# Attention scores without a wide reciprocal, a first chunk that starts its MLP alone, and weights fetched from the beginning

## The chip, the cores and the metric

The kernel runs on one core of one Trainium2 chip. The metric is device time in microseconds (us) of one execution; lower is better. All times are medians of runs in the fast state on the chip (an execution over 1.5% above the fastest of its kernel would be left out), each with runs of the kernel before beside it.

## The reference

An attention layer with a decaying state (RWKV-6) for 4 sequences, 8 heads, 768 steps, head size 48, and after it an MLP with a hard-swish gate:

```python
for t in range(S):                       # per batch and head
    cur = outer(u * k_t, v_t)
    y_t = r_t @ (state + cur)
    state = w_t[:, None] * state + outer(k_t, v_t)
x = y, heads side by side                # (3072, 384)
h = x @ w_in                             # (384, 2048)
g = h * clip(h + 3, 0, 6) / 6
out = g @ w_out                          # (2048, 384)
```

## The kernel before

The steps are cut into 24 chunks of 128 (6 to a sequence). Within a chunk the products of decays turn the recurrence into matrix products: R = r times the decay up to the step, K = k divided by the decay up to and with the step, and the scores are K against R. Three chunks make a block of 384 columns (the tile xT) for the MLP, with 16 up projections ("ups", three matmuls of 384 columns each, then a gate on ScalarE and VectorE) and 12 quarters of a down projection. The weights arrive as 64-bit words and are converted on ScalarE and VectorE, in pairs of 128-column slices: 16 conversions. PSUM is the memory that the matmuls write their results to. All this is interleaved; in each built program every engine has its own fixed list of instructions.

```python
def weights(which, f):                         # fetch a pair and convert it
    ...
    bits = io.tile([128, n], I64, name="bits", bufs=3)
    ...                                        # two DMAs on SyncE's queue
    nc.scalar.activation(out=more, in_=lo, ...)          # 2 on ScalarE
    nc.scalar.activation(out=more.bitcast(I32), in_=more, ...)
    nc.vector.tensor_scalar(out=top, in0=hi, ...)        # 3 on VectorE
    nc.vector.scalar_tensor_tensor(out=top, in0=hi, ...)
    nc.vector.tensor_tensor(out=dst, in0=top, in1=more.bitcast(I32), op=ALU.add)

def prep(i):
    d = st[i]
    W_ = wk.tile([PR, P * (L + 1)], F32, name="W")
    nc.vector.tensor_tensor_scan(out=W_, data0=d["w"], data1=restart..., op0=ALU.mult, op1=ALU.add)
    ...
    nc.vector.reciprocal(out=inv, in_=W[:, :, 1:])       # 112 x 512
    ...
    nc.gpsimd.tensor_mul(R, d["r"], W[:, :, :L])
    nc.gpsimd.tensor_mul(K, d["k"], inv)
    ...                                        # rk on GpSimd, dg on VectorE, A on ScalarE

def up(bk, f):
    h_ps = pp.tile([128, MB], F32, name="mm", bufs=4)    # one of four PSUM buffers
    for j in range(NCC):
        nc.tensor.matmul(h_ps, lhsT=w_in[:, f, j, :], rhs=b["xT"][:, j, :], ...)
    r6 = wk.tile([128, MB], F32, name="r6", bufs=3)
    nc.scalar.activation(out=r6, in_=h_ps, func=ACT.Relu, bias=half, scale=1.0 / 6.0)
    nc.vector.scalar_tensor_tensor(out=g, in0=r6, scalar=1.0, in1=h_ps, op0=ALU.min, op1=ALU.mult)

def attend(i, some=lambda n: None):            # score: K against R, then the mask on VectorE
    score(i); turn_k(i); some(3); write(i); some(1); read(i)   # some(n): n pieces of the MLP

prep(0); prep(1); attend(0); prep(2); attend(1); attend(2)
first = pieces_of(0)                           # 16 ups, 12 quarters of a down
...                                            # 3 conversions ahead of the first up, the rest spread over the ups
todo.extend(first)
load(3); prep(3)
...
for i in range(BC, NT):
    left = max(0, (i - BC + 1) * per_block // BC - lag - done)   # lag = 5
    ...
    load(i + 1); attend(i, some); prep(i + 1); some(left)
```

## Time and profile before

| | before |
|---|---|
| median of 3 runs | 647.87 us (647.71 to 648.11) |
| span of the profiled run | 647.6 us (a run of 649.35 us), mean granted clock 0.982 |
| TensorE busy | 609.8 us (94%) |
| VectorE busy | 318.8 us (49%) |
| GpSimd busy | 135.7 us (21%) |

The prediction below shows the slices, the timeline and the stretches. Two more views are needed later. First the groups of instructions of the page: line, engine, operation, tiles written and read, count, then busy time and mean ns of one, then idle time of the engine before them and what ended it.

```profile
L211 DVE RECIPROCAL inv<-W 112x512 f32<-112x512 f32 x24 | 80.4, 3349 | 0.6
...
L215 POOL TENSOR_TENSOR K<-feat_in,inv 112x512 f32<-112x512 f32 x24 | 31.1, 1296 | 57.9 <-DVE inv L211 36.1
```

The wide reciprocal costs 3.35 us a chunk, a quarter of VectorE's busy time, and GpSimd's K waits for it. The second view is what TensorE waited for in the first 125 us (us in total, times, longest).

```profile
PE a_ps L234 <- POOL K L215: 17.8, 3, 15.5
```

Of 17.8 us for K, 15.5 are the start of the program.

### The profile page before, as it was taken

How to read it: one execution, taken by the hardware profiler on the slowest of the kernel's cores; microseconds unless marked ns; L12 is line 12 of the kernel's file. 1: busy time of each engine (PE TensorE's matmuls, PEld its weight loads, DVE VectorE, ACT ScalarE, POOL GpSimd, SP SyncE). 2: the span in 40 equal slices, each digit the busy share in tenths (PEclk: the TensorE clock that was granted, in tenths of full speed). 3: DMA queues.
4: the chain of work that ended last, by engine and by line, in shares of the span. 5: the costliest groups of instructions: out<-in, count | busy, mean ns of one | idle time of the engine just before them, and what ended most of it. 6: DMA issues, size and time to landing. Idle time of an engine off the chain costs nothing.

```text
span 647.6 us, 7143 instructions
## 1 busy us (share of the span) xinstructions
PE 609.8 (94%) x2706; PEld 383.2 (59%) x2706; DVE 318.8 (49%) x366; ACT 215.6 (33%) x517; POOL 135.7 (21%) x124
## 2 busy tenths in 40 slices
PE   0688989999999999999999999999999999999996
PEld 0564555666556666666666666666666666555553
DVE  4899999789873651145431852134530533002200
ACT  1576856143321443033320443132430432102200
POOL 5734233231131321031130420121220200000000
PEclk9889969999999999999999999999999999999999
DMA  8939786998760413030130322011100000000000
GB/s 234 284 92 312 261 267 232 287 315 294 239 197 17 130 37 90 24 92 21 60 100 14 92 80 72 30 53 51 37 10 24 14 1 0 22 25 0 2 13 28
DMA packets 23578, 67.24 MB, mean 104 GB/s; under 512 B 2800, under 2 KB 12912, under 8 KB 23536
## 3 DMA queue, kind: packets, MB, share of 16 engines
q1 hardware_dynamic: 23536, 66.70, 33.1%
q8 instruction: 23, 0.38, 0.2%
q14 instruction: 19, 0.16, 0.1%
HBM read 60.79 MB, written 4.72 MB: 101 GB/s over the span
## 4 chain that ended last, share of the span: by engine, by line
PE 80%; DVE 9%; DMA 3%; POOL 3%; issue 2%; ACT 1%; SPq 0%; DVEq 0%; POOLq 0%; ACTq 0%
PE mm L328 37%; PE mm L310 32%; PE a_ps L234 3%; PE ps L292 3%; PE ps L287 2%; DVE inv L211 2%; PE ps L259 2%; DMA bits<-in_wflat_dram 1%; PE ps L248 1%; DVE W L207 1%; DVE w_in L99 1%; DVE top L97 1%; DMA bits<-in_moe_w_in_dram 1%; DMA feat_in<-in_feat_dram 1%; POOL K L215 1%
## 5 line engine op out<-in xcount | busy, mean ns | idle before, releaser
L310 PE MATMUL mm<-xT,w_in 128*128 128x384 f32 x768 | 258.3, 492 | 2.8 <-DVE g L315 2.8
L328 PE MATMUL mm<-w_out,g 128*128 128x384 f32 x768 | 255.1, 488 | 0.0
L310 PEld LDWEIGHTS mm<-xT,w_in 128*128 128x128 f32 x768 | 144.0, 191 | 100.8 <-DVE g L315 5.2
L328 PEld LDWEIGHTS mm<-w_out,g 128*128 128x128 f32 x768 | 143.6, 190 | 96.5 <-issue 2.4
L315 DVE SCALAR_TENSOR_TENSOR g<-r,mm 128x384 f32<-128x384 f32 x128 | 69.3, 550 | 114.7 <-ACT r L313 114.4
L313 ACT ACTIVATE r<-mm,half 128x384 f32<-128x384 f32 x128 | 73.7, 579 | 141.3 <-PE mm L310 137.8
L211 DVE RECIPROCAL inv<-W 112x512 f32<-112x512 f32 x24 | 80.4, 3349 | 0.6
L271 POOL TENSOR_TENSOR S<-base,W 112x448 f32<-112x448 f32 x20 | 20.1, 1007 | 241.5 <-DVE base L269 191.9
L225 ACT ACTIVATE A<-ident,dg 128x128 f32<-128x128 f32 x192 | 60.3, 389 | 7.1 <-DVE dg L221 6.8
L237 DVE COPY_PREDICATED A<-mask,a_ps 128x1024 f32<-128x1024 uint8 x24 | 31.3, 1306 | 47.7 <-PE a_ps L234 47.6
L234 PE MATMUL a_ps<-R,K 48*128 48x128 f32 x384 | 30.4, 298 | 17.8 <-POOL K L215 17.8
L234 PEld LDWEIGHTS a_ps<-R,K 48*128 48x128 f32 x384 | 25.4, 198 | 30.5 <-POOL K L215 18.7
L215 POOL TENSOR_TENSOR K<-feat_in,inv 112x512 f32<-112x512 f32 x24 | 31.1, 1296 | 57.9 <-DVE inv L211 36.1
L207 DVE TENSOR_TENSOR_SCAN W<-feat_in,restart 112x516 f32<-112x516 f32 x24 | 34.4, 1434 | 17.8 <-POOL S L271 12.7
L214 POOL TENSOR_TENSOR R<-feat_in,W 112x512 f32<-112x512 f32 x24 | 31.5, 1314 | 48.8 <-DVE W L207 40.7
L332 ACT COPY o<-mm 128x384 f32<-128x384 f32 x24 | 11.5, 478 | 86.0 <-PE mm L328 85.9
L216 ACT COPY w_min<-W 112x4 f32<-112x4 f32 x24 | 4.7, 197 | 99.0 <-DVE W L207 99.0
L221 DVE TENSOR_REDUCE dg<-rk 128x8 f32<-128x384 f32 x24 | 13.0, 542 | 49.4 <-POOL rk L219 49.3
L218 POOL TENSOR_TENSOR rk<-tok_in 128x384 f32<-128x384 f32 x24 | 26.3, 1097 | 41.7 <-DMA tok_in<-in_tok_dram 40.7
L297 ACT COPY xT<-ps 48x384 f32<-48x384 f32 x48 | 22.7, 472 | 28.7 <-PE ps L292 28.3
L250 ACT COPY kn<-ps 128x448 f32<-128x448 f32 x20 | 10.6, 530 | 57.5 <-PE ps L248 57.4
L259 PE MATMUL ps<-tok_in,kn 128*112 128x96 f32 x160 | 21.4, 283 | 7.7 <-ACT kn L250 7.7
(46 smaller groups left out, 308.6 us busy)
## 6 DMA issues: line engine op xcount, KB each, us to landing
feat_in<-in_feat_dram SPq DMA_DIRECT2D x24, 673.8 KB, 5.1
tok_in<-in_tok_dram SPq DMA_DIRECT2D x24, 576.0 KB, 4.9
bits<-in_moe_w_in_dram SPq DMA_DIRECT2D x16, 384.0 KB, 6.2
bits<-in_moe_w_out_dram SPq DMA_DIRECT2D x16, 384.0 KB, 4.0
bits<-in_moe_w_in_dram SPq DMA_DIRECT2D x8, 768.0 KB, 5.9
bits<-in_moe_w_out_dram SPq DMA_DIRECT2D x8, 768.0 KB, 5.5
bits<-in_wflat_dram SPq DMA_DIRECT2D x6, 768.0 KB, 5.9
out_dram<-o SPq DMA_DIRECT2D x24, 192.0 KB, 1.9
```

The source lines that it names most:

```text
L207: nc.vector.tensor_tensor_scan(out=W_, data0=d["w"], data1=restart.rearrange("q p t -> q (p t)"), initial=0.0, op0=ALU.mult, op1=ALU.add)
L211: nc.vector.reciprocal(out=inv, in_=W[:, :, 1:])
L214: nc.gpsimd.tensor_mul(R, d["r"], W[:, :, :L])
L215: nc.gpsimd.tensor_mul(K, d["k"], inv)
L225: nc.scalar.activation(out=A[:, h, :], in_=ident, func=ACT.Copy, scale=dg[:, h])
L234: nc.tensor.matmul(a_ps[:, g, p, :], lhsT=d["K"][rows, p, :], rhs=d["R"][rows, p, :], start=True, stop=True)
L237: nc.vector.copy_predicated(out=d["A"].rearrange("s (p g) t -> s g p t", g=2), mask=mask.rearrange("s (o x t) -> s o x t", o=1, x=1).to_br ...
L259: nc.tensor.matmul(kv_ps[:, p].rearrange("q g e -> q (g e)"), lhsT=d["kn"][:, p, :], rhs=d["v"][:, 2 * p:2 * p + 2, :].rearrange("s h e -> ...
L310: nc.tensor.matmul(h_ps, lhsT=w_in[:, f, j, :], rhs=b["xT"][:, j, :], start=(j == 0), stop=(j == NCC - 1))
L313: nc.scalar.activation(out=r6, in_=h_ps, func=ACT.Relu, bias=half, scale=1.0 / 6.0)
L315: nc.vector.scalar_tensor_tensor(out=g, in0=r6, scalar=1.0, in1=h_ps, op0=ALU.min, op1=ALU.mult)
L328: nc.tensor.matmul(o_ps, lhsT=b["g"][f][:, c * L:(c + 1) * L], rhs=w_out[:, f, :], start=(f == 0), stop=(f == NFC - 1))
```

## The change

Three parts. (a) The wide reciprocal goes: a scan that runs backward over w gives E, the decay from a step to the chunk's end; K = k times E; the forward scan then starts at one over the chunk's whole decay (a reciprocal of 4 columns), so that R carries the inverse. In the first three chunks the multiplies and the state's decay are moved from GpSimd to VectorE. (b) The fetch of weights is parted from their conversion, and the first three fetches are issued from the beginning. (c) The first chunk's columns are moved into xT by themselves, so that the first block's ups run as 128 columns (chunk 0) and later 256 (chunks 1 and 2); the conversions of w_out stand in pairs ahead of the first quarters of the down projection. With them comes a split of the first chunk's load, whose w third is now a transfer of its own.

For the traces below: in the changed kernel tile E holds K after its multiply, and tile W holds R; kn is K turned, a_ps the scores in PSUM, mm the PSUM buffers of the ups and downs, g the gates.

```diff
-    def weights(which, f):
+    def fetch(which, f): ...
+    def convert(which, f): ...
@@ load
+            if i == 0:
+                nc.sync.dma_start(out=a[:, 2 * n:], in_=feat[i, :, 2 * n:])
+                nc.scalar.dma_start(out=a[:, :2 * n], in_=feat[i, :, :2 * n])
@@ after load(1)
-        load(2)
+        fetch_next()
+        load(2)
+        fetch_next()
+        fetch_next()
@@ prep
-            nc.vector.tensor_tensor_scan(out=W_, data0=d["w"], data1=restart..., ...)
-            nc.vector.reciprocal(out=inv, in_=W[:, :, 1:])
-            nc.gpsimd.tensor_mul(R, d["r"], W[:, :, :L])
-            nc.gpsimd.tensor_mul(K, d["k"], inv)
+            eng = nc.vector if i < BC else nc.gpsimd
+            nc.vector.tensor_tensor_scan(out=E_[:, ::-1], data0=d["w"][:, :0:-1], data1=back...[:, ::-1], ...)
+            nc.vector.reciprocal(out=start[:, :, 0:1], in_=E[:, :, 0:1])
+            nc.vector.tensor_tensor_scan(out=W_, data0=d["w"][:, :-1], data1=start..., ...)
+            K, R = E[:, :, 1:], W[:, :, :L]
+            eng.tensor_mul(K, d["k"], K)
+            eng.tensor_mul(R, d["r"], R)
@@ read
-            if c == BC - 1:
+            if c == BC - 1 or i == 0:
+                cols = slice(0 if i == 0 or bk > 0 else L, (c + 1) * L)
@@ up
-        def up(bk, f):
+        def up(bk, f, c0=0, c1=BC):        # columns c0*L to c1*L, its own PSUM buffer, its own gate
@@ the beginning
-        prep(1)
         attend(0)
+        prep(1)
+        convert_next()
+        attend(1)
+        up(0, 0, 0, 1)
+        up(0, 1, 0, 1)
         prep(2)
-        attend(1)
+        convert_next()
+        up(0, 2, 0, 1)
+        up(0, 3, 0, 1)
+        convert_next()
         attend(2)
-        ...                                # conversions spread over the ups
+        load(3)
+        first = [(up, 0, 4, 0, 1), (up, 0, 5, 0, 1)]
+        rest = [(up, 0, f, 1, BC) for f in range(NFC)]
+        for f in range(6, NFC, 2):
+            first += rest[:2] + [(convert_next,), (up, 0, f, 0, 1), (up, 0, f + 1, 0, 1)]
+            del rest[:2]
+        for q in range(QD):
+            first += rest[:2] + [(convert_next,), (convert_next,), (down, 0, q)]
+            del rest[:2]
+        first += [(down, 0, c) for c in range(QD, BC * QD)]
```

(Cut: the constants, the state's decay as a step of its own, the second program path, the layout of the inputs.)

## The prediction

> **What bounds the kernel now.** I read the page's slices first, then TensorE's instructions in order of time, then VectorE's in the same stretch, then the busy time by stretches.
>
> The page, busy tenths in 40 slices of 16.2 us, with the granted clock and the DMA rate below:
>
> ```profile
> PE   0688989999999999999999999999999999999996
> ...
> DVE  4899999789873651145431852134530533002200
> ...
> PEclk9889969999999999999999999999999999999999
> ...
> GB/s 234 284 92 312 261 267 232 287 315 294 239 197 17 130 37 90 24 92 21 60 100 14 92 80 72 30 53 51 37 10 24 14 1 0 22 25 0 2 13 28
> ```
>
> TensorE is full from about slice 6 on, and VectorE is full only before that. So the end is the time at which TensorE becomes full plus the work then left, and whatever helps must lie in the first 100 us. TensorE's timeline there (start us, duration us, what):
>
> ```profile
> 15.52 2.08 PE L234 MATMUL a_ps<-R,K 48*128 48x128 f32 x16 [15.52 <-POOL K L215]
> ...
> 34.36 1.16 PE L234 MATMUL a_ps<-R,K 48*128 48x128 f32 x16
> ...
> 47.95 8.01 PE L310 MATMUL mm<-xT,w_in 128*128 128x384 f32 x24
> 57.65 1.16 PE L234 MATMUL a_ps<-R,K 48*128 48x128 f32 x16 [1.69 <-POOL K L215]
> ...
> 83.14 2.05 PE L287 MATMUL ps<-R,S 112*112 112x128 f32 x8 [3.61 <-POOL R L214]
> 85.76 1.64 PE L234 MATMUL a_ps<-R,K 48*128 48x128 f32 x10 [0.57 <-POOL K L215]
> 87.33 4.21 PE L310 MATMUL mm<-xT,w_in 128*128 128x384 f32 x6
> ```
>
> The first score starts at 15.5 us; no up projection starts before 47.95, since all need the block of three chunks. The stretches (PE, PEld, DVE, ACT, POOL busy us, granted clock, DMA share, GB/s):
>
> ```profile
> 0.00:47.95 47.95, 24.48 (x200) 20.99 (x200) 36.60 (x38) 22.55 (x59) 27.71 (x29) 0.89 0.72 205
> 47.95:87.33 39.38, 31.99 (x144) 20.29 (x143) 39.19 (x44) 29.20 (x57) 15.77 (x11) 0.93 0.88 284
> ...
> 194.47:268.81 74.34, 74.34 (x338) 46.68 (x338) 29.98 (x32) 23.41 (x60) 15.15 (x14) 1.00 0.21 62
> ```
>
> From 48 to 87 VectorE is busy 39.2 of 39.4 us and TensorE waits for it. A full block of three chunks takes 74.3 us and needs 30 us of VectorE.
>
> **A ledger of TensorE's full-speed work.** In the full stretches of the chain of waits a record of 128x384 takes 5.82/18 = 0.323 us; there are 6 to an up and 8 to a quarter of a down, so a block has 192, or 62.0 us. One chunk's attention is 1.09 (score) + 0.44 (turning K) + 0.77 (outer products) + 0.88 (reading the state) + 1.01 (reading A) = 4.2 us. Lost time is elapsed time less such work:
> - To 47.95: four scores and turns 6.1, three products 2.3, two state reads 1.8, three A reads 3.0 = 13.2 of work; lost 34.7.
> - 47.95 to 87.33: 72 records 23.2, attention 5.8 = 29.0 of 39.4; lost 10.4.
> - 87.33 to 101.08: 32 records and 0.4 = 10.7 of 13.75; lost 3.0, as the clock is half until about 92.
> - Later 1.5 (a wait of 0.99 at 163 and small ones). Together 49.6 us.
> Total work is 1536 x 0.3225 + 92 = 587.6; the tail after the last matmul at 641.9 is 5.7. The sum, 643, leaves 4.7 of small gaps that I take to stay.
>
> **What the Trainium skill says.**
> - "VectorE: DVE Perf Modes", section "First, the fixed hardware budget", gives reciprocal as an iterative divide with a repeat count of 8. The trace agrees that it is dear, not on 8: 3.35 us for 512 elements is 6.3 cycles each at the page's 0.96 GHz. The scan takes 1.23 us for 516.
> - The same page, "Mode 1× (REGULAR) — the baseline": one result a cycle for fp32 with two tensors. No such 512-wide VectorE multiply is in this trace; the 128x384 one of g takes 0.55 us with one operand in PSUM, so I estimate 0.65 for 512.
> - "GPSIMD Engine Reference", "1. Specifications": GpSimd's SBUF interfaces are shared with VectorE and contended by instructions with two SBUF inputs or in a 2-port mode. The trace agrees: the scan takes 1.23 us alone, 1.75 to 2.0 beside GpSimd; the conversion's first operation 0.55 alone, up to 1.43.
> - "TensorE: Matmul & The Clock Gate", "What's actually happening": half clock after an idle window of about 3.4 us, full after as long a busy one. The trace shows 2.08 us for the first score and 1.09 to 1.16 when warm, and half clock after the gap of 3.6 us before 83.14.
>
> **The change part by part.**
>
> *Reciprocal.* Removed per chunk: 3.35 us on VectorE. Added: a second scan, 1.23, and a reciprocal of 4 columns, about 0.1. In the first three chunks the two multiplies (about 1.3 together; on GpSimd 1.2 to 4.4 each) and from the second on the state's decay (about 0.55) also move to VectorE. So VectorE per chunk goes from 1.23 + 3.35 + 0.5 + 1.3 + 0.7 = 7.1 to about 6.9 in the first three and to 5.1 afterwards: 2.0 saved per chunk from chunk 3 on, less if GpSimd slows both scans. What the first chunks gain is latency: scan, reciprocal, GpSimd multiply was 5.85 at best, and for chunk 0 it was 6.65 to 15.5 because R on GpSimd took 4.41 and rk stood ahead of K. Now 1.23 + 0.1 + 1.23 + 1.3 = 3.9. The w third of the first load is a transfer of its own; I put its landing at 4.5 to 5 instead of 6.6. First score then at about 8.7: 6.8 us earlier.
>
> *Weights from the beginning.* The first pair is now queued before load 2 and two more behind it. In order of bytes (1.28 MB a chunk, 0.79 a pair, 240 to 290 GB/s as in the first 20 us) the pairs land at about 16.5, 24 and 27 us; before they were issued at 24.4 and first converted at 40.4. This fills the DMA hole (52, 0 and 39 GB/s between 36 and 48 us), which is worth about 9 us of transfer, and lets three conversions of 2.75 us (0.89 + 0.95 + 0.95; 2.3 with overlap) use VectorE's early idle time of 11 us.
>
> *First chunk alone.* With chunk 0's columns copied at about 22 us, six ups of 128 columns run before the block is whole: 6 x 6 records x 0.11 (as the 128-column state read) = 4 us of TensorE's work, in time that was idle. Extra cost of splitting 384 into 128 + 256: 96 extra matmul records, a few ns each, and 16 extra gate operations on VectorE of 0.15, together near 1 us.
>
> *The block whole.* VectorE up to chunk 2's masking now has 3 preparations of 4.3 (with dg), 3 maskings 3.9, products 1.4, decay 1.1, conversions 7, gates 0.8 = 27; from 4.7 with some 5 idle that is 37. Reading, copies and the partition-moving transfers took 8.5 after the masking before (39.4 to 47.95) and stay so unless the masking is early: the 256-column ups start between 37 and 44, say 40.5. Work done then: 11.7 (three chunks, no state read in the first) + 1.5 + 4 = 17.2. Lost 23.3 instead of 34.7: 11.4 gained.
>
> *From there to the last conversion.* VectorE has 13 conversions x 2.3 = 30, attention 3.3 chunks x 5.1 = 17, gates 7.5, contention: about 54, so to about 94 (before: last conversion 105.4). TensorE meanwhile has ups 31 - 4 = 27, three quarters of a down 7.7, attention 11 = 46. Lost 6 to 8, and I add 2 for one half-clock spell. Then 9 quarters of a down are ready and TensorE stays full. Against 10.4 + 3.0: 4 to 5 gained. Sum: 49.6 becomes 23.3 + 9 + 1.5 = 34, about 15.5 us less; 647.9 - 15.5 = 632.4, which I put at 633 for the split's cost.
>
> **The rivals.**
> (1) *VectorE's early work binds the first block anyway.* Its load per early chunk hardly falls (7.1 to 6.9), conversions now stand before chunk 2 in the program, and the static order may put them before its masking. For it: VectorE is 93% busy from 24 to 48 already. Against: 11 us of idle before 48, though 6.6 of it is the wait for the first data. Then the block is whole at 45 and the gain is 7 to 9: 639 to 641.
> (2) *The down projection's conversions pile up.* The new order puts eight of them (18 to 22 us) between chunk 5's and chunk 6's score, where TensorE has about 20 us; with 6.3 MB of weights and a load at 280 GB/s that takes 27 us. Lost there could be 10 and a half-clock spell on top: 638 to 642.
> (3) *Everything fits*: masking of chunk 2 near 31, ups from 37, VectorE uncontended: 626.
> (4) *Slower*: later blocks are bounded by TensorE, with VectorE at 40% and falling, so only a bad order of DMA issue (a fetch waiting for its buffer ahead of load 3) could cost; it would eat the gain rather than exceed it.
>
> **Range and chances.** The middle is 633; (1) and (2) together partly cancel the gain, (3) bounds it. Range 626 to 641. The 2% mark is 634.9, just above my middle: faster 0.6, same 0.39, slower 0.01.
>
> **What would show it.** First score at 8 to 10 us; the 128-column ups between 22 and 40; the 256-column ups from 37 to 44; no hole in the DMA rate before 80 us; last conversion of w_out at 90 to 98; block periods after that still 74.3. I am wrong if the 256-column ups start as late as 47, if TensorE waits more than 12 us in all between 45 and 110, or if the period of the later blocks changes.

## The result

The changed kernel took 648.66 us (648.07 to 650.32, 4 runs), the kernel before 647.79 us (646.96 to 648.11, 4 runs) in the same rounds. The ratio is 1.002, with a 95% interval of 0.9998 to 1.0041: the same. A ratio here is the mean time of one kernel's runs over the mean of the other's of the same rounds, so it is not quite the ratio of the medians. The prediction of 633 and its range (626 to 641) missed.

The page of the changed kernel, slices of 16.2 us:

```profile
PE   2667997999999999999999999999999999999996
...
DVE  7988999769853343314412434115520133002200
...
PEclk9898999999999999999999999999999999999999
...
GB/s 261 192 228 258 221 221 246 325 273 315 285 241 34 71 81 54 48 104 34 48 101 14 91 80 35 66 62 0 38 9 25 13 1 1 21 26 0 1 14 28
```

The start is busier, and the hole in the DMA rate (92 in the third slice before) is filled. But slice 7 (97 to 113 us) has a dip in TensorE that was not there before. TensorE's timeline (start us, us, what, idle time before and what ended it):

```profile
11.48 2.08 PE L270 MATMUL a_ps<-W,E 48*128 48x128 f32 x16 [11.48 <-DVE W L251]
...
31.68 1.60 PE L355 MATMUL mm<-xT,w_in 128*128 128x128 f32 x12
...
46.70 2.08 PE L270 MATMUL a_ps<-W,E 48*128 48x128 f32 x16 [3.13 <-POOL W L251]
...
51.19 4.56 PE L355 MATMUL mm<-xT,w_in 128*128 128x256 f32 x24
...
109.42 13.57 PE L374 MATMUL mm<-w_out,g 128*128 128x384 f32 x36 [3.40 <-DVE w_out L106]
```

The first score came 4 us earlier than before (11.48 against 15.52). The first ups of 128 columns ran from 31.68. But the ups of 256 columns started at 51.19, later than the whole ups before (47.95). Chunk 3's score, at 46.70, waited 3.13 us and ran at half speed: 2.08 us against the 1.16 of a warm one. Then the down projection waited 3.40 us for a conversion and ran 36 matmuls in 13.57 us, where full speed needs 36 x 0.323 = 11.6. TensorE's waits from 26 to 112 us:

```profile
PE a_ps L270 <- POOL W L251: 5.5, 2, 3.1
PE mm L374 <- DVE w_out L106: 3.4, 1, 3.4
PE ps L284 <- POOL E L250: 3.0, 2, 1.6
```

And the two scans and GpSimd's multiply, from the page:

```profile
L250 POOL TENSOR_TENSOR E<-feat_in,E 112x512 f32<-112x512 f32 x21 | 26.6, 1266 | 191.3 <-issue 108.8
...
L246 DVE TENSOR_TENSOR_SCAN W<-feat_in,start 112x516 f32<-112x516 f32 x24 | 38.7, 1614 | 15.0 <-PE ps L329 14.8
...
L239 DVE TENSOR_TENSOR_SCAN E<-feat_in,back 112x516 f32<-112x516 f32 x24 | 29.3, 1219 | 3.7 <-DMA feat_in<-in_feat_dram 3.7
```

The backward scan takes the 1.22 us that were expected. The forward scan runs beside GpSimd's multiplies (rk, K or the decay), and in the first 120 us its nine instances took 1.92 us each. So the pair of scans with the small reciprocal (0.18) cost 3.3 us there, against 1.57 + 3.34 = 4.9 before.

The ledger of the prediction, filled in for the changed kernel: TensorE had lost 32.8 us when the 256-column ups began, then 14.0 more. That is 46.8, against 34 predicted and 49.6 before. (The profiled run before took 649.35 us, 1.5 above its median, and that of the change 648.07, 0.6 below: so the smaller sum is no gain in time.) For the 14.0, the span of 646.3 is lessened by the prediction's 587.6 of work, 5.7 of tail and 4.7 of small gaps, by the 32.8, and by 1.5 for the split's extra matmul records. The 1.5 is a rough estimate: where halves alternate, 24 of them (12 pairs) took 4.20 to 4.30 us, and 12 whole matmuls 4.03 (e12) and 4.14 (e16), so all 96 pairs cost 0.5 to 2.2 us more.

### The profile page after: what moved, and what is told of

The parts are those of the page before. It is cut to its first block, busy times and chain, and to the rows that moved or that the text cites. A ratio compares the mean times of both kernels' runs of the same rounds, so it can differ in the third digit from the quotient of the medians.

```text
span 646.3 us, 7370 instructions
## 1 busy us (share of the span) xinstructions
PE 608.9 (94%) x2802; PEld 392.8 (61%) x2802; DVE 284.0 (44%) x414; ACT 216.8 (34%) x533; POOL 126.3 (20%) x118
## 4 chain that ended last, share of the span: by engine, by line
PE 86%; DVE 6%; DMA 2%; ACT 2%; issue 1%; POOL 1%; ACTq 0%; SPq 0%; DVEq 0%
PE mm L374 38%; PE mm L355 35%; PE ps L334 3%; PE a_ps L270 3%; PE ps L329 2%; PE ps L295 2%; DMA feat_in<-in_feat_dram 1%; PE ps L284 1%; DVE top L102 1%; DVE w_out L106 1%; DVE W L246 1%; DVE top L104 1%; DMA bits<-in_moe_w_out_dram 1%; DVE g L361 1%; DVE E L239 1%
## 5 line engine op out<-in xcount | busy, mean ns | idle before, releaser
L355 PE MATMUL mm<-xT,w_in 128*128 128x384 f32 (+2 forms) x864 | 258.7, 454 | 1.9 <-DVE g L361 1.3
L361 DVE SCALAR_TENSOR_TENSOR g<-r,mm 128x384 f32<-128x384 f32 (+2 forms) x144 | 71.8, 505 | 132.2 <-ACT r L358 131.9
L358 ACT ACTIVATE r<-mm,half 128x384 f32<-128x384 f32 (+2 forms) x144 | 77.7, 544 | 126.2 <-PE mm L355 124.4
L250 POOL TENSOR_TENSOR E<-feat_in,E 112x512 f32<-112x512 f32 x21 | 26.6, 1266 | 191.3 <-issue 108.8
L270 PE MATMUL a_ps<-W,E 48*128 48x128 f32 x384 | 30.6, 303 | 16.9 <-DVE W L251 11.5
L246 DVE TENSOR_TENSOR_SCAN W<-feat_in,start 112x516 f32<-112x516 f32 x24 | 38.7, 1614 | 15.0 <-PE ps L329 14.8
L270 PEld LDWEIGHTS a_ps<-W,E 48*128 48x128 f32 x384 | 25.7, 204 | 28.1 <-DVE W L251 11.5
L334 PE MATMUL ps<-A,tok_in 128*48 128x128 f32 x384 | 27.7, 289 | 4.2 <-DVE A L273 4.2
L239 DVE TENSOR_TENSOR_SCAN E<-feat_in,back 112x516 f32<-112x516 f32 x24 | 29.3, 1219 | 3.7 <-DMA feat_in<-in_feat_dram 3.7
L255 POOL TENSOR_TENSOR rk<-rk,u_bc 128x384 f32<-128x384 f32 x24 | 27.9, 1162 | 1.7
```

The costliest lines, as they stand in the source:

```text
L239: nc.vector.tensor_tensor_scan(out=E_[:, ::-1], data0=d["w"][:, :0:-1], data1=back.rearrange("q p t -> q (p t)")[:, ::-1], initial=0.0, op ...
L246: nc.vector.tensor_tensor_scan(out=W_, data0=d["w"][:, :-1], data1=start.rearrange("q p t -> q (p t)"), initial=0.0, op0=ALU.mult, op1=ALU ...
L255: nc.gpsimd.tensor_mul(rk, rk, u_bc)
L270: nc.tensor.matmul(a_ps[:, g, p, :], lhsT=d["K"][rows, p, :], rhs=d["R"][rows, p, :], start=True, stop=True)
L334: nc.tensor.matmul(y_ps[g * GP:g * GP + D, p, :], lhsT=d["v"][:, h, :], rhs=d["A"][:, h, :], start=(first and p == 0), stop=(p == P - 1), ...
L355: nc.tensor.matmul(h_ps[:, :n], lhsT=w_in[:, f, j, :], rhs=b["xT"][:, j, cols], start=(j == 0), stop=(j == NCC - 1))
```

## The experiments

All runs gave correct results. The ratio is always to the kernel before of the same call. The calls were e1 to e4, e5 to e8, e9 to e11, e12 to e15 and e16 to e18; the median of the kernel before was 648.15, 648.39, 647.52, 647.64 and 647.29 us in them. Where kernels of different calls are compared, medians and ratios differ by up to 1.2 us, and the ratios are the fairer. By the mark of 2% every run but e5 is the same as the kernel before, and e5 is unclear; what follows rests on the intervals.

| run | kernel | median us | ratio (95%) |
|---|---|---|---|
| e1 | change, loads 3 and 4 issued early | 650.41 | 1.0035 (1.0022 to 1.0047) |
| e2 | before + (a) alone | 643.42 | 0.9924 (0.9908 to 0.9940) |
| e3 | before + (b) alone | 647.77 | 0.9989 (0.9966 to 1.0012) |
| e4 | (a) + (b), block whole | 641.00 | 0.9887 (0.9871 to 0.9903) |
| e5 | change, conversions evenly paced | 659.18 | 1.0185 (1.0151 to 1.0218) |
| e6 | e4, conversions as late as in the change | 645.66 | 0.9964 (0.9950 to 0.9977) |
| e7 | e4, all multiplies on VectorE | 638.79 | 0.9866 (0.9845 to 0.9886) |
| e8 | e5 + loads early | 654.40 | 1.0094 (1.0074 to 1.0114) |
| e9 | e4, all ups of block 0 split in place | 650.41 | 1.0049 (1.0027 to 1.0070) |
| e10 | e4, chunk 0's columns moved early | 643.19 | 0.9925 (0.9905 to 0.9944) |
| e11 | e7 + four ups alone, loads early | 637.89 | 0.9858 (0.9834 to 0.9882) |
| e12 | e4, only the gates split | 646.86 | 0.9997 (0.9973 to 1.0021) |
| e13 | e9, halves share a PSUM buffer | 657.87 | 1.0155 (1.0137 to 1.0173) |
| e14 | e9, all multiplies on VectorE | 648.78 | 1.0013 (0.9989 to 1.0038) |
| e15 | e7 + loads early | 642.78 | 0.9908 (0.9875 to 0.9941) |
| e16 | e4, chunk 5's score two ups earlier | 644.76 | 0.9961 (0.9945 to 0.9977) |
| e17 | e9, chunk 5's score held back | 648.53 | 1.0019 (1.0001 to 1.0036) |
| e18 | change, all multiplies on VectorE | 642.20 | 0.9926 (0.9910 to 0.9942) |

### Which part gains: e1 to e4

After the first reading I had three theories. A: the fetches, which wait for one of three buffers, stand ahead of load 3 in the DMA queue (chunk 3's first load was issued at 31.7 us, before at 15.5). B: VectorE's early work binds, whatever the loads do. C: the first chunk alone is worth its 4 us.

**e1**, the loads put ahead of the waiting fetches:

```diff
         prep(0)
+        load(3)
         attend(0)
         prep(1)
+        load(4)
         ...
-        load(3)        # after attend(2); and the loop loads from chunk 5 on
```

> The changed kernel, with the loads of chunks 3 and 4 put ahead of those weight fetches that wait for a free buffer; nothing else edited. Theory A (the change lost its gain to the order on the load queue: chunk 3's data was issued at 31.7 us instead of 15.5, and TensorE's order has chunk 3's score ahead of the 256-column ups): chunk 3's score below 40 us instead of 46.7, 256-column ups from about 44 instead of 51.2, time 638 to 642. Theory B (VectorE's early work binds, whatever the loads do): time within 2 of the changed kernel's 648.

Chunk 3's load was issued at 19.8 us and chunk 4's at 30.1. The waits for GpSimd's R are gone from the list, and others have taken their place: this one, and 3.8 us each for gates and for conversions of w_out. The second line is from the timeline:

```profile
PE ps L295 <- ACT kn L286: 7.7, 3, 4.5
...
56.99 4.11 PE L355 MATMUL mm<-xT,w_in 128*128 128x256 f32 x24
```

The time is 0.15% longer than the change's, by the ratios. A has fallen. Chunk 3's score came at 42.71 us (A: below 40), but the 256-column ups only at 56.99 (A: from 44): more of the attention now stands ahead of them in TensorE's list, and it waited 4.5 us for chunk 3's kn.

**e2**: the kernel before, with only the new prep (both scans, the small reciprocal, the first three chunks' multiplies on VectorE) and the decay step.

> The kernel before with the arithmetic of the change alone (second scan for the wide reciprocal, multiplies of the first three chunks on VectorE); loads, fetches and the first block as before. Theory A: a gain of its own, since VectorE has 2 us less per chunk from chunk 3 on and the first score comes 4 us earlier: 641 to 644. Theory B's form of it (the scan with two inputs is slowed by GpSimd to 2 us and the saving is lost): 646 to 649.

**e3**: the kernel before, with only fetch parted from conversion and issued from the beginning.

> The kernel before with the early fetches alone (wide reciprocal kept, block taken whole). The loads of chunks 3 and 4 stand ahead of the waiting fetches here. Theory A: the DMA hole at 36 to 48 us closes and the ups no longer wait for conversions as long: 643 to 646. Theory B (VectorE is full from 24 us on, so weights that are there earlier are not converted earlier): 647 to 649.

**e4**: both, with the block whole and the conversions where they were before:

```diff
+        prep(0); prep(1); attend(0); prep(2); attend(1); attend(2)
+        first = pieces_of(0)                    # whole ups
+        first[p] = convs[before:upto] + first[p]  # as before, convs = [(convert_next,)] * 16
-        ...                                     # all of part (c)
```

> The changed kernel without its middle part: backward scan and early fetches, but block 0 taken whole as before, and loads 3 and 4 ahead of the waiting fetches. Theory A: the first chunk alone is what pulled the late loads in and brought little itself: 637 to 641. Theory C (the first chunk alone is worth its 4 us of TensorE work): slower than the run with early loads by 3 to 5. Theory B: 645 or more.

The scan alone takes 0.0076 x 648 = 4.9 us off; the fetches alone take nothing that can be told from zero; both together take 7.3 off. So what e4 leaves out, which was meant to gain, costs 7.7 us by the medians (648.7 against 641.0) and 8.6 by the ratios, and C has fallen; so has B, which had 645 or more for e4. What e4 leaves out is part (c), the split of the first load and the late place of loads 3 and 4. The loads' place is not it (e1); the split of the load was not run by itself, but the first score came at 12.00 us without it against 11.48. The ledger says where (c) costs. e4's timeline:

```profile
42.03 2.08 PE L266 MATMUL a_ps<-W,E 48*128 48x128 f32 x16 [4.98 <-POOL W L247]
...
47.37 8.80 PE L351 MATMUL mm<-xT,w_in 128*128 128x384 f32 x24
```

Chunk 3's score waits for GpSimd's R here too, for 4.98 us. In e4 the whole ups begin at 47.37 with 14.9 us of work done (four scores, turns and products, three reads), so 32.5 lost; the change had lost 32.8 at 51.19. The six early ups just make up for the later start. After that e4 lost 7.4 in all (637.9 - 587.6 - 5.7 - 4.7 - 32.5), the change 14.0. So against e4, (c) costs its time after the block has begun.

### Late conversions or split ups: e5, e6, e8

Theory D: the conversions of w_out stand too late (the last ended at 109.4 us; at 97.0 in e4). Theory E: splitting the ups costs by itself.

**e5**, the change with the conversions spread over the ups:

```diff
-        first = [(up, 0, 4, 0, 1), ...]         # conversions late, in pairs
+        for p in range(NFC):                    # about one conversion, then both halves of up p
+            first.append([(convert_next,)] * (upto - since)
+                         + [(up, 0, p, 0, 1)] * (p >= 4) + [(up, 0, p, 1, BC)])
```

> The changed kernel with the first chunk alone kept (all 16 ups split 128 + 256), but the conversions spread over the ups as in the kernel before (about one per up) instead of five among the ups and eight in pairs between the last ups and the first downs. Theory D (the change loses because its conversions come late: the last one ends at 109 us, against 97 with the block whole): 640 to 643, last conversion before 101. Theory E (the splitting itself costs: each up becomes two, in the in-order queues of TensorE, ScalarE and VectorE, and the first chunk's columns need transfers of their own): 647 or more, whatever the pace.

**e6**, e4 with its conversions as late as in the change; TensorE's list of instructions is the same as in e4:

```diff
-            first[p] = convs[before:upto] + first[p]
+        for p, k in [(0, 3)] + [(f, 1) for f in range(6, NFC, 2)] + [(NFC + q, 2) for q in range(QD)]:
+            first[p] = [(convert_next,)] * k + first[p]
```

> The run with backward scan and early fetches and the block whole (641.0), with nothing but the conversions moved as late as in the change: three first, one before every second up from the seventh on, two before each of the first four quarter downs. TensorE's static order is the same as in that run. Theory D: 646 to 649, with TensorE waiting for conversions of the down weights. Theory E: within 2 of 641.

e6 costs 4.7 us against e4 by the medians (5.0 by the ratios), and its waits name the reason:

```profile
PE mm L370 <- DVE w_out L106: 5.7, 3, 2.6
```

e4 has no such wait. So late conversions cost (D), in a whole block. But e5, which mends just that, is 10.5 us slower than the change. Its waits are for the attention (the profiled run took 665.1 us, 5.9 above e5's median, so they are larger than usual):

```profile
PE a_ps L270 <- POOL W L251: 10.4, 3, 3.6
PE ps L284 <- POOL E L250: 6.0, 1, 6.0
```

I read it so: an even pace puts more conversions ahead of the preparation of the next chunks on VectorE, and with split ups TensorE then has too little to do until K and R come, where with whole ups (e4) it has enough. No run tests this by itself. **e8**, e5 with e1's early loads, tells how much of that is the loads:

> As the first run of this call, with the loads of chunks 3 and 4 ahead of the waiting fetches as well. Theory D with A as a second cause: 2 to 4 faster than the first run of this call. If the loads cost nothing, within 1.5 of it.

It took 654.4: the loads are 4.8 us of it, and it is still slower than the change. So D is shown only with whole ups, and E stands.

### What the split costs: e9, e10, e12, e13, e14, e16, e17

**e9**, e4 with each up of the first block as two, in the same place:

```diff
-        first = pieces_of(0)
+        first = [[(up, 0, f, 0, 1), (up, 0, f, 1, BC)] for f in range(NFC)] + pieces_of(0)[NFC:]
```

> The run with scan and early fetches (641.0), with every up of block 0 split into 128 and 256 columns where it stands, one right after the other; no chunk goes alone, nothing else moves. Theory E1 (twice the gate operations is what the splitting costs: on ScalarE 0.37 + 0.47 us for 0.58, on VectorE 0.28 + 0.40 for 0.55, each with its own wait): 643 to 646. Rival E2 (the cost comes from where the 128-column ups stand, between attention and the other ups in in-order queues): within 1.5 of 641.

It costs 9.4 us against e4 by the medians (10.5 by the ratios), though the sum of columns is the same. TensorE's timeline, e4 first:

```profile
69.19 8.01 PE L351 MATMUL mm<-xT,w_in 128*128 128x384 f32 x24
78.64 2.20 PE L351 MATMUL mm<-xT,w_in 128*128 128x384 f32 x6 [1.44 <-DVE g L357]
80.84 1.16 PE L266 MATMUL a_ps<-W,E 48*128 48x128 f32 x16
83.45 6.07 PE L351 MATMUL mm<-xT,w_in 128*128 128x384 f32 x18 [1.45 <-DVE g L357]
```

And e9 (a mixed group is named by its first shape; the 24 are halves of both widths):

```profile
70.25 4.30 PE L351 MATMUL mm<-xT,w_in 128*128 128x128 f32 x24
80.98 1.22 PE L266 MATMUL a_ps<-W,E 48*128 48x128 f32 x6 [6.43 <-POOL W L247]
...
84.86 7.31 PE L351 MATMUL mm<-xT,w_in 128*128 128x256 f32 x30
```

In both, chunk 5's score starts at 81 us. e4 has 13 ups behind it by then, e9 has 10: its fixed list has the score earlier, and TensorE waits 6.43 us there. What VectorE does in that gap of e9:

```profile
72.53 0.41 DVE L357 SCALAR_TENSOR_TENSOR g<-r,mm 128x256 f32<-128x256 f32 x1
...
77.07 1.96 DVE L242 TENSOR_TENSOR_SCAN W<-feat_in,start 112x516 f32<-112x516 f32 x1
...
79.81 0.27 DVE L357 SCALAR_TENSOR_TENSOR g<-r,mm 128x128 f32<-128x128 f32 x1
```

From 72.9 to 79.8 it makes no gate, but two scans of chunk 5 and parts of conversions. The granted clock after the gap (columns as in the prediction, the clock is third from the end):

```profile
80.00:82.00 2.00, 1.02 (x6) 0.93 (x6) 2.00 (x4) 1.21 (x2) 0.93 (x1) 0.50 0.43 118
...
88.00:90.00 2.00, 2.00 (x11) 1.87 (x11) 1.55 (x4) 1.31 (x3) 0.00 (x0) 0.85 0.60 240
```

In the stretches between these it is 0.50 too, so half clock lasts until about 88.6. The cost adds up: waits of 6.43 and 0.80 against e4's 2.89, 4.3; 7.6 us at half clock, 3.8; the estimate of 1.5 for more records; together 9.6, against 10.0 between the two profiled spans (647.9 and 637.9).

**e10**, e4 with chunk 0's columns moved into xT early, ups whole:

```diff
-            if c == BC - 1:
+            if c == BC - 1 or i == 0:
```

> The same base, with chunk 0's columns moved by their own early transfers on two queues as in the change, all ups whole. Theory E3 (the early transfers hold up ScalarE, which waits 2 us in its queue to issue three of them, and the load queue, where chunk 3's load now stands behind them): 643 to 645. Rival: within 1.5 of 641.

It cost 2.2 us by the medians (2.5 by the ratios), as much as E3 had, but whether for E3's reason I did not check. In its trace the ups begin at 48.58 us instead of 47.37, and a wait of 3.69 us for a gate before 81.68 is followed by matmuls at half clock (6 in 4.21 us). The early transfers are not free, but they are the smaller part.

Three theories for the 9.4. G: the extra gate instructions on ScalarE and VectorE. P: each half holds one of the four PSUM buffers, so that four halves (4.3 us of TensorE's work) are all that it can do while gates are late, where four whole ups are 8.0 us. S: the place of chunk 5's score in the fixed list.

**e12**, matmuls whole, only the gates split:

```diff
+            for c0, c1 in ((0, 1), (1, BC)) if bk == 0 else ((0, BC),):
+                nc.scalar.activation(out=r6[:, :n], in_=h_ps[:, cols], ...)
+                nc.vector.scalar_tensor_tensor(out=b["g"][f][:, cols], in0=r6[:, :n], in1=h_ps[:, cols], ...)
```

> The kernel with the backward scan and the early fetches and the whole first block (641.0), but in the first block each gate is computed in two pieces, 128 and 256 columns, while the matmuls stay 384 wide and each up keeps one PSUM buffer. The run with matmuls and gates split and a buffer for each half was 650.4, 9.4 slower. Theory G (the extra gate instructions cost it: 24 more on ScalarE and on VectorE, by the durations there 0.26 and 0.13 us more for each up, 6.2 and 3.1 us in all): 646 to 650. Theory P (each half holds one of the four PSUM buffers, so that only two ups are in flight): 641 to 643. Theory S (the order in which the instructions were laid down on TensorE, chunk 5's score after 10 ups instead of 13): here the score stands after 12 ups, so 641 to 644.

5.9 us slower than e4 by the medians, 7.1 by the ratios. That is in G's range (though its sum counts 24 more instructions where the edit adds 16 on each engine, so 4.2 and 2.1 us instead of 6.2 and 3.1), but the score stood after 12 ups instead of 13, and TensorE waited 2.9 us for R at 81.7 and three times 0.7 to 1.0 before it, with the granted clock at 0.86, 0.90 and 0.82 in the three stretches of 12 us from 60 to 96. The lost clock alone is at most 12 x (0.14 + 0.10 + 0.18) = 5 us. So e12 does not part G from S.

**e13**, e9 with both halves in one PSUM buffer (one h_ps for an up, columns c0 to c1 of it):

> The same kernel with matmuls and gates of the first block split 128 and 256, but the two halves of an up in one PSUM buffer. G: 646 to 650, for the gate instructions are there. P: 641 to 644, as four ups are in flight again. S: the order on TensorE is changed once more at build: chunk 5's first five score matmuls stand after all 128-column parts and the other three behind part of the first down projections, so no early wait for chunk 5; but one weight load more for each 128-column matmul. S then expects 641 to 646, and that the wait of TensorE for chunk 5's R at about 75 us is gone.

It took 657.9, the slowest but e5. TensorE's list was changed again at build, and it waited for gates nine times (8.3 us from 45 to 125 us). It is no clean test of P. Halves with more PSUM buffers, which would be one, were not run.

**e14**, e9 with the multiplies of every chunk on VectorE:

```diff
-            eng = nc.vector if i < BC else nc.gpsimd
+            eng = nc.vector
```

> The kernel with every up of the first block split in place and a PSUM buffer for each half (650.4), but with all multiplies of the attention on VectorE, as in the run that gave 638.8 with whole ups. TensorE's order still has chunk 5's score early, after 10 ups. Theory S in its narrow form (the loss is the 6.4 us wait for GpSimd's R multiply at 75 us and the half clock after it): the wait falls below 2 us and the time to 640 to 643. Theories G and P: the split costs its 9 us here too, 646 to 649.

648.8: GpSimd's slowness is not what the split costs. R came from VectorE at 79.8, hardly earlier, and TensorE still waited 3.84 us for it.

**e16**, e4 with two ups moved behind chunk 5's attention and nothing split:

```diff
-            left = max(0, (i - BC + 1) * per_block // BC - lag - done)
+            left = max(0, (i - BC + 1) * per_block // BC - lag - (3 if i == 2 * BC - 2 else 0) - done)
```

> The kernel with scan and early fetches and the first block whole (641.0), with one thing moved: two up projections are laid down behind chunk 5's attention instead of ahead of it, so that on TensorE chunk 5's score stands after 11 whole ups instead of 13. No instruction is added or split. Chunk 5's R came at about 80 to 82 us in every run that I looked at. Theory S (the fixed order costs: TensorE reaches the score with nothing else that it may do, waits and then runs at half clock): about 2 ups more, 4 us, are held back behind the score, a wait for R of 4 to 6 us at about 76 us and half clock after it, 645 to 650. Theory G (the extra gate instructions): no change, 640 to 642.

```profile
66.59 6.07 PE L351 MATMUL mm<-xT,w_in 128*128 128x384 f32 x18
80.06 2.08 PE L266 MATMUL a_ps<-W,E 48*128 48x128 f32 x16 [7.40 <-POOL W L247]
82.06 7.52 PE L351 MATMUL mm<-xT,w_in 128*128 128x384 f32 x18
```

The order alone costs 0.0074 x 647 = 4.8 us (3.8 by the medians), with the same wait and half clock. S is shown to cost time, though a bit less than I expected (645 to 650).

**e17**, e9 with the score held back (behind 15 ups by its trace, where the expectation says 14), by adding 0 times a gate to one element of R:

```diff
+            if i == 2 * BC - 1:
+                g, R = blocks[0]["g"][8], st[i]["R"]
+                nc.vector.scalar_tensor_tensor(out=R[0:1, 0, 0:1], in0=g[0:1, MB - 1:MB], scalar=0.0, in1=R[0:1, 0, 0:1], op0=ALU.mult, op1=ALU.add)
```

> The kernel with every up of the first block split in place (650.4), but chunk 5's score held back: one element of its R is added to 0 times one element of the ninth up's gate, on VectorE, which leaves R as it is and at build puts the score after 14 ups instead of 10. All split matmuls and gates stay. S: the wait of 6.4 us for R is gone and with it the half clock from 81 to 92 us; 641 to 645. G: the extra gate instructions still cost, 647 to 651. Both in part: 645 to 647.

```profile
70.59 4.20 PE L351 MATMUL mm<-xT,w_in 128*128 128x128 f32 x24
80.78 1.65 PE L351 MATMUL mm<-xT,w_in 128*128 128x128 f32 x6 [5.99 <-DVE g L357]
```

By the ratios 1.9 us better than e9, not the 6 to 9 of S. The score is out of the way, and TensorE stops at nearly the same moment (74.8 us against 74.6), after the same 24 matmuls, now for a gate. In e4 four whole ups from 69.19 lasted until 77.2. So two things limit TensorE at this place, and taking one away shows the other: the score at the head of the list, and four PSUM buffers that are full because VectorE makes no gate until 80. Behind both lies VectorE's list, which is busy without a gap in this stretch in e4 too (12.00 of 12.00 us from 72 to 84). That four halves bridge 4.2 us and four wholes 8.0 is what e17 and e4 show. How much of the 9.4 the extra gate instructions add by themselves stays open.

### What is left to gain: e7, e11, e15, e18

**e7**, e4 with all multiplies and the decay on VectorE (the edit of e14):

> The run with scan and early fetches (641.0), with the multiplies of K and R and the decay on VectorE in every chunk instead of the first three. Theory F (GpSimd slows VectorE's instructions with two inputs: the forward scan took 1.9 us on average to 105 us against 1.22 for the backward one): scans fall to 1.25, VectorE gains 1.3 us of work per chunk and loses as much of slowing, chunks 3 to 5 come through earlier, 637 to 640. Rival: VectorE is the bound there and 1.9 us per chunk more on it costs 3 to 5: 644 to 646.

**e11**, e7 with four ups of chunk 0 alone ahead of and behind chunk 2's attention, the rest whole, and loads 3 and 4 early:

> The run with all multiplies on VectorE (638.8), with chunk 0 alone through the first four ups only, two conversions ahead of chunk 2's attention, loads 3 and 4 at the front, the other twelve ups whole and the conversions paced as before. If the idea of the first chunk alone is sound once its costs are kept small: 635 to 637. If the early 128-column ups only displace other work: 638 to 641.

**e15**, e11 without its four ups alone:

> The best run so far (637.9: all multiplies on VectorE, four ups of the first chunk alone, loads 3 and 4 early) without its four ups alone. If even four ups alone pay, this is slower by 1 to 2 us than 637.9; if they pay nothing, it lies within 1 us of it; if the early loads are what gained there, it is at or below 637.9 and below 638.8, the run without early loads.

e7 is 2.2 us faster than e4 by the medians and 1.4 by the ratios, whose intervals overlap, and e11 is equal to e7 within the intervals. e15 is slower than both (runs from 638.5 to 645.3; its interval just overlaps theirs): early loads alone seem to lose here, and four ups alone to bring some 3 us back (0.9908 - 0.9858). Why the early loads would lose I did not find. The best kernel is e11 at 637.89, 1.4% under the kernel before; e7 is as good, and simpler.

**e18**, the change itself with the edit of e14:

> The change as it is, with all multiplies of the attention on VectorE (the change has those of chunks 3 onward on GpSimd). In the change TensorE waited 5.5 and 3.0 us for GpSimd's R and K of chunks 3 and 4. If GpSimd is what holds these chunks: both waits halve and the time is 641 to 645. If VectorE's own work is what holds them (scans and conversions in one queue, as the run with split ups and all on VectorE suggests with 648.8): waits of the same size for VectorE's R and 645 to 649.

642.2: 6.1 us better than the change by the ratios, where the same edit gained 1.4 in the whole block (e7). From 26 us on TensorE's waits are now:

```profile
PE mm L374 <- DVE w_out L106: 3.8, 4, 1.4
PE ps L284 <- DVE E L250: 1.6, 1, 1.6
PE a_ps L270 <- DVE W L251: 1.6, 1, 1.6
```

The waits for R and K of chunks 3 and 4, 8.5 us in the change, are 3.2, and the longest of all waits is 1.6 instead of 3.4. The down projection's four waits do not drop the clock. So in the change GpSimd's multiplies stood on the path, and the edit that takes them away wins back most of the 8.6 us that separate it from e4. They also slow the forward scan, which took 1.22 us in e14 against 1.70 in e9 (means from 45 to 110 us).

## Why the prediction was wrong, point by point

- **First score, 8.7 us predicted, 11.48 measured.** Mis-sized. The w third of the load was to land at 4.5 to 5; the backward scan started at 6.1. The forward scan took 2.05 instead of 1.23 and the R multiply 1.30 instead of 0.65, both beside GpSimd's rk.
- **The block whole, 40.5 predicted, 51.2 measured: the step that failed.** It is 9.5 us of the ledger (23.3 against 32.8). The working had VectorE at chunk 2's masking until 37 us and 8.5 us from there to the ups, which makes 45.5; I wrote 40.5, the middle of a range "between 37 and 44". The masking ended at 36.7, as worked out, and the last column transfer was issued at 44.0 and took 1.8 to 2.6 us, so that the columns were there at about 46. The rest, to 51.2, is a path that the working lacked: chunk 3's score and outer products and half of its state read stand ahead of the 256-column ups in the fixed list, the score waited for GpSimd's R until 46.7, and the clock was half until about 52. The working had score and turn as 1.5 us of work, without a wait and at full clock.
- **From there to the last conversion, 94 predicted, 109 measured.** 14.0 lost against 9 and 1.5. The terms that the working names (30, 17 and 7.5) already make 54.5, so the contention that it lists was given nothing; the nine forward scans of the first 120 us alone took 6.3 us more than at 1.22. Rival 2 had this one: conversions pile up. e6 puts it at 4.7 us in a whole block, and GpSimd's multiplies are the other part that runs show (e18).
- **The split's cost, "near 1 us".** As extra work on TensorE it is 0.5 to 2.2. In place it cost 9.4 (e9). What the prediction lacked is that an up is also TensorE's store of work: four PSUM buffers of whole ups bridge 8 us of a VectorE that is busy elsewhere, four halves bridge 4. In the change itself, though, TensorE's ups waited only 1.3 us for gates from 26 to 112 us, against 8.5 for GpSimd's R and K: the buffers show in e17's wait for a gate, and how much of the change's own loss is theirs is not shown.
- **Reciprocal, 2.0 us saved a chunk.** Right in kind: 1.6 in the first 120 us, and e2 alone gained 4.9 us of time. **Weights from the beginning**, "worth about 9 us of transfer": right as transfer, but no time by itself (e3).
- **Rivals.** (2) came true, and of (1) the late block but not its reason: VectorE's masking ended when the middle had it. I had let each take part of the gain. (4) said that a bad order of DMA issue would eat the gain; the order was there, and e1 shows that it was not the cause.
- **The later blocks** did not change, as predicted: from chunk 9's score to the end 453.2 us before and 453.0 after. Of my marks for being wrong, the first was met (256-column ups later than 47), the second nearly: TensorE was idle for 10.3 us from 45 to 110.
- **Readings and sums.** "VectorE is full only before that" is not so: in the kernel before VectorE was busy 12.00 of 12.00 us from 96 to 108 and from 108 to 120, when TensorE was full as well. The total work is 587.4 by its own terms, not 587.6; the 0.2 falls to the small gaps and changes no difference.

So the 15 us went like this: (a) and (b) gained 7.3 (e4), half of what I gave to all three; (c), with the split of the first load, cost 8.6 by the ratios (7.7 by the medians), and with the multiplies on VectorE about 4 (e18 against e7, 0.9926 against 0.9866). Why those 4 remain is open.

## What to carry to other kernels

A unit of work that is cut in two also halves what the engine can do ahead in a fixed number of buffers; before splitting, look at how long the consumer is busy elsewhere and whether the buffers bridge it (here 4.2 us instead of 8.0, in e17 and e4). An instruction at the head of a fixed list that waits holds up ready work behind it (7.40 us in e16), so look at what stands behind each wait. When a working gives a number, use it, and do not replace it by the middle of a hoped-for range.

## What the Trainium skill lacked or had wrong

- "VectorE: DVE Perf Modes", section "First, the fixed hardware budget": gives reciprocal a repeat count of 8, but no time; the 112x512 one took 3.35 us, 6.3 cycles an element at the page's 0.96 GHz. The 112x4 one took 0.18 us.
- "GPSIMD Engine Reference", section "1. Specifications": says that the two engines contend; the section itself has no figure. The backward scan took 1.22 us and the forward one, beside GpSimd, 1.92 on average to 120 us (1.22 in e14, without GpSimd's multiplies), and with all multiplies on VectorE the change was 6 us faster (e18).
- "TensorE: Matmul & The Clock Gate", section "What's actually happening": gives full speed after at least one busy window of about 3.4 us. In the change half clock began only after the restart at 109.4 us and lasted 3.4 us (0.54 from 110 to 112 us, 0.61 to 114, then 1.00), so full clock came back 4.2 us after the restart; in e9, with work that never paused after 81.0 us, half clock lasted 7.6 us from the restart, more than two such windows.
- No page that I found says how many buffers of PSUM are needed to bridge a consumer that is busy elsewhere: here four of 384 columns bridged 8.0 us and four halves 4.2.
